# Loading and turning z earlier, and a regrouped start, in a gated attention kernel with a maxout layer

## The chip, the cores and the metric

The kernel runs on one core of a Trainium2 chip. The metric is the device time of one execution in microseconds, and lower is better. Five engines work beside each other: PE (TensorE, matrix products into PSUM), DVE (VectorE), ACT (ScalarE), POOL (GpSimd) and SP (SyncE). Here POOL and SP mostly issue transfers, each from a queue of its own that is served in order.

## The reference, cut to what matters

There are B = 8 sequences of S = 3072 rows. z has 64 columns, u and v have 256, and w1 and w2 are 256 x 1024.

```
scores = z @ z.T / S                     # one 3072 x 3072 matrix for each sequence
attn   = maximum(scores, 0) ** 2
x      = u * (attn @ v)
out    = maximum(x @ w1, x @ w2) @ w_out
```

scores is symmetric, so a block below the diagonal is a turned block from above it.

## The kernel before

**Tiles.** S is cut into 24 blocks of 128 rows, and four blocks make a chunk of 512 queries. One `Step` (b, s) does chunk s of sequence b, six for each sequence and 48 in all. A step adds up 24 blocks k of attn @ v into two PSUM tiles `xacc` (256 rows of D, 512 queries). Its result times u (`epilogue`, L299) is `xT`, which goes through the maxout layer (`d_ps`, `g_sb`, `o_ps`, `o_sb`) three steps later (LAG = 3), so that TensorE always has products at hand.

**Scores.** `scores_pair` (from L220 on) makes the scores of two blocks k0, k0 + 1 for the 512 queries of a step, from `zT`, the turned z: two products, run beside each other on the two halves of the rows. ACT takes the maximum with zero (`r_sb`, L233; DVE at L231 for two pairs of the head), DVE squares it (`a_sb`, L236). If the block lies above the diagonal, SP issues a DMA transpose of it (`aT`), which a later step of the same sequence uses; in the first sequence steps 0 to 3 compute each other's blocks directly instead (`direct`). From step 4 on the four diagonal blocks are made by `scores_diag`: only the upper half is computed and three small DMA transposes fill the rest (`aD`). `s_ps`, `d_ps`, `o_ps` and the transposes `tpz` of the start share three PSUM buffers (`mm_psum`).

**z.** For each sequence z is loaded by POOL (`load_z`, cast to bf16) and turned by two DMA transposes on SP (`make_zT`). The first sequence's z alone is turned by TensorE (`zT_pe`, L149), and its result is copied by DVE or ACT (L150).

**The planner.** `work` lists TensorE's products in order, with planned times from their lengths. Scores have no planned length: they are put in between as windows of up to three pairs (`scores_window`). Each window is placed, from the last to the first, at the last place that suits the due times of its tiles: the planned time of the first use less LAT_OWN, LAT_TURNED or LAT_DIAG (L536), or 2592 ns in the first steps. The three windows of the very start are written out by hand (`ahead`, `squared`, `third`), with products of zeros (`idle`) between them. `transfers` holds loads and transposes with planned times. A load is put behind a small copy on POOL (`gate`, L98) that waits for the newest square or other fresh result, so that it is not issued too early. A transpose is only queued on SP.

**Start.** Nine blocks of z (ZF) come through SP in fp32 and are cast by DVE and ACT, the other 15 come through POOL, then v in six groups of four blocks and u.

Of the kernel before, what the change touches and what calls it, by code (L numbers as in the profile page):

```python
# [11 lines left out]
def kernel(  # L12
# [19 lines left out]
    nc = tc.nc  # L32
    fp32 = mybir.dt.float32
    bf16 = mybir.dt.bfloat16
# [4 lines left out]
    dqk = z.shape[-1]  # L39
    Dff = moe_w1.shape[-1]  # L40

    P = 128
    H = P // 2
    NSB = S // P
    G = 4
    WIN = 3
    GW = G * P
# [10 lines left out]
    consts = ctx.enter_context(tc.tile_pool(name="consts", bufs=1))  # L58
    zepool = ctx.enter_context(tc.tile_pool(name="zepool", bufs=1))
# [11 lines left out]
    mm_psum = ctx.enter_context(tc.tile_pool(name="mm_psum", bufs=3, space=bass.MemoryType.PSUM))  # L71
    acc_psum = ctx.enter_context(tc.tile_pool(name="acc_psum", bufs=1, space=bass.MemoryType.PSUM))

    pin = tc.keep_in_program_order

    def matmul(*args, **kw):
        return pin(nc.tensor.matmul(*args, **kw))  # L77
# [13 lines left out]
    def sp_dma(**kw):  # L91
        pin(nc.sync.dma_start(**kw))
# [7 lines left out]
    def load(**kw):  # L100
        pin(nc.gpsimd.dma_start(**kw))  # L101
# [19 lines left out]
    def load_v(b, v_sb, t0, n):  # L121
        load(
            out=v_sb[:, ds(t0, n), :],
            in_=v[b].rearrange("(p t) d -> p t d", p=P)[:, ds(t0, n), :],
        )

    def load_u(b, c):
        u_sb = ulpool.tile([P, G, D], bf16, name="u_sb")
        load(
            out=u_sb,  # L130
            in_=u[b].rearrange("(p t) d -> p t d", p=P)[:, ds(c * G, G), :],
        )
        return u_sb
# [10 lines left out]
    def zT_pe(zT, z_sb, s0, n, tpz=None):  # L144
        flat = z_sb.rearrange("p t d -> p (t d)")
        if tpz is None:
            tpz = mm_psum.tile([P, 8, P], bf16, name="tpz", tag="mm")
        for j in range(n):
            pin(nc.tensor.transpose(tpz[:, j, :], flat[:, ds((s0 + j) * dqk, P)], ident))  # L149
        return lambda copy: pin(copy(zT[:, ds(s0, n), :], tpz[:, :n, :]))  # L150
# [68 lines left out]
    def scores_pair(b, s, k0):  # L219
        q = seqs[b]  # L220
        s_ps = mm_psum.tile([P, 2, GW], fp32, name="s_ps", tag="mm")
        for j in range(2):
            score(q, s_ps[:, j, :], j, k0 + j, s, 0, G)
        yield
        a_sb = apool.tile([P, 2, GW], bf16, name="a_sb")
        r_sb = apool.tile([P, 2, GW], bf16, name="r_sb", bufs=3)

        head = b == 0 and s == 0 and k0 < 12
        keep = pin if head else lambda ins: None
        if head and k0 in (2, 10):  # L230
            keep(nc.vector.tensor_single_scalar(out=r_sb, in_=s_ps, scalar=0.0, op=ALU.max))  # L231
        else:
            keep(nc.scalar.activation(r_sb, s_ps, AF.Relu))  # L233
        if head:
            yield
        keep(nc.vector.tensor_mul(a_sb, r_sb, r_sb))  # L236
        gj = k0 // G
        if gj > s and not direct(b, s, gj):
            if (s, gj) not in q.T:
                q.T[s, gj] = tpool.tile([P, G, G, P], bf16, name="aT")  # L240
            turn(
                q.T[s, gj][:, ds(k0 - G * gj, 2), :, :].rearrange("p k q x -> p (k q) x"),
                a_sb.rearrange("p j q -> p (j q)"),
            )
        yield a_sb
# [149 lines left out]


    q = seqs[0]
    ZF = 9
    blank = consts.tile([P, GW], bf16)
    pin(nc.vector.memset(blank, 0.0))  # L400
    zf = opool.tile([P, G, D], fp32, name="o_sb").rearrange("p t (n d) -> p (t n) d", d=dqk)
    z_in = z[0].rearrange("(p t) d -> p t d", p=P)
    sp_dma(out=zf[:, :ZF, :], in_=z_in[:, :ZF, :])
    ident = consts.tile([P, P], bf16)
    make_identity(nc, ident)
    z_sb_0 = zepool.tile([P, NSB + 2, dqk], bf16, name="z_sb")
    pin(nc.gpsimd.memset(z_sb_0[:, 0:1, :], 0.0))
    pin(nc.gpsimd.memset(z_sb_0[:, NSB + 1 : NSB + 2, :], 0.0))
    load(out=z_sb_0[:, 1 + ZF : 1 + NSB, :], in_=z_in[:, ZF:, :])
    pin(nc.vector.tensor_copy(z_sb_0[:, 1:6, :], zf[:, :5, :]))  # L410
    pin(nc.scalar.copy(z_sb_0[:, 6 : 1 + ZF, :], zf[:, 5:ZF, :]))
    q.v = new_v()
    for t0 in range(0, NSB, G):
        load_v(0, q.v, t0, G)
    q.u_sb[0] = load_u(0, 0)
    q.zT = zpool.tile([P, NSB + 1, P], bf16, name="zT")


# [111 lines left out]
    steps = [Step(b, s) for b in range(B) for s in range(NG)]  # L530
# [2 lines left out]


    work = []
    LAT_OWN, LAT_TURNED, LAT_DIAG = 3500, 9000, 12000  # L536

    def put(ns, shares, fn, reads=()):
        work.append((ns, shares, fn, reads))
# [9 lines left out]
    def put_block(st, k):  # L549
        row = NG * st.b + st.s  # L550
        if k // G in st.early:
            reads = [((NG * st.b + k // G, k0), LAT_TURNED) for k0 in (G * st.s, G * st.s + 2)]
            put(216, False, lambda: st.add_early(k), reads)
        elif k // G == st.s and st.diag:
            put(216, False, lambda: st.add_diag(k % G), [((row, None), LAT_DIAG)])
        else:
            put(216, False, lambda: st.add_own(k), [((row, k - k % 2), LAT_OWN)])

# [127 lines left out]
    while True:  # L686
# [4 lines left out]
            break  # L691
        windows.insert(0, [tiles.pop()])
        places.insert(0, i)
    firsts = [tiles[i : i + 2] for i in range(0, 6, 2)]
    firsts += [tiles[i : i + WIN] for i in range(6, len(tiles), WIN)]
    for rows in reversed(firsts):
        places.insert(0, lay(rows, GAP_FIRST))
    windows = firsts + windows
# [34 lines left out]
    for n, st in enumerate(steps):  # L733
        b, s = st.b, st.s
        if n + 1 < len(steps):
            nx = steps[n + 1]
            plan_load(b, s, 5 if st.halves else 2, lambda nx=nx: fetch_u(nx.b, nx.s))
        plan(b, s, 1, False, lambda b=b, s=s: turn_u(b, s))
        if s == 0 and b + 1 < B:
            c = b + 1  # L740
            if b == 0:
                z_at, zT_at = (3, 5), (4, 4)
                v_at = [(4, 8), (4, 14), (5, 1), (5, 6), (5, 11), (5, 15)]
            else:
                z_at, zT_at = (0, 7), (3, 3)
                v_at = [(s, 14) for s in range(NG)]
            plan_load(b, *z_at, lambda c=c: fetch_z(c))
            plan(b, *zT_at, False, lambda c=c: turn_z(c))
            for i, at in enumerate(v_at):
                plan_load(b, *at, lambda c=c, i=i: fetch_v(c, i))  # L750
# [7 lines left out]
    def scores_window(w):  # L758
        gens = []
        for n, k0 in windows[w]:  # L760
            st = steps[n]
            make = scores_diag(st.b, st.s) if k0 is None else scores_pair(st.b, st.s, k0)
            gens.append((st, k0, make))
        for st, k0, gen in gens:
            next(gen)
        for st, k0, gen in gens:
            st.scored[k0] = a = next(gen)
            fresh[0] = a[:, 0, 0:1] if k0 is not None else a[:, 0, 0, 0:1]
# [3 lines left out]

    def idle(n):
        for _ in range(n):
            matmul(steps[0].xacc[0], blank[:, :P], blank, start=True, stop=True)


    laid = {i: [w for w in ws if w > 2] for i, ws in laid.items()}
    idle(6)
    parts = [zT_pe(q.zT, z_sb_0, 0, 5), zT_pe(q.zT, z_sb_0, 5, ZF - 5)]  # L780
    for part, copy in zip(parts, (nc.vector.tensor_copy, nc.scalar.copy)):
        part(copy)
    idle(4)
    heads = {k0: scores_pair(0, 0, k0) for w in range(3) for _, k0 in windows[w]}

    def ahead(*k0s):
        for k0 in k0s:
            next(heads[k0])

    def squared(*k0s):  # L790
        for k0 in k0s:
            steps[0].scored[k0] = a = next(heads[k0])
            fresh[0] = a[:, 0, 0:1]

    ahead(0, 2)
    ahead(0, 2)
    tpz = mm_psum.tile([P, 2, 8, P], bf16, name="tpz", tag="mm")
    parts = [zT_pe(q.zT, z_sb_0, ZF + 8 * i, 8, tpz[:, i]) for i in range(2)]
    squared(0)
    for part, copy in zip(parts, (nc.scalar.copy, nc.vector.tensor_copy)):  # L800
        part(copy)
    ahead(4)
    idle(1)
    ahead(6)
    idle(2)
    ahead(4, 6)
    squared(2, 4)

    def third():
        ahead(8, 10)  # L810
        ahead(8, 10)
        squared(6, 8, 10)

    laid.setdefault(spots[0] + 2, []).insert(0, -1)
    for i, (_, _, fn, _) in enumerate(work):
        for w in laid.get(i, []):
            scores_window(w) if w >= 0 else third()
        while transfers and transfers[0][0] <= begins[i]:
            _, _, is_load, begin_transfer = transfers.pop(0)
            if is_load:  # L820
                gate(fresh[0])
            begin_transfer()
        fn()
# [30 lines left out]
```

## Time and profile before

| | us |
|---|---|
| median of 3 runs | 977.18 (976.05 to 978.23) |
| profiled execution | 974.66 |
| its span in the trace | 972.9 |
| PE busy in the span | 956.9 |
| ACT busy | 485.9 |
| DVE busy | 391.5 |

PE is busy for 98% of the span. The rest of the profile is read stretch by stretch: a wait of PE is named with what ended it last, and times are microseconds from the start of the span. The granted clock of the profiled run is 0.996 as a mean.

### The profile page before, as it was taken

To read this page: it belongs to the slowest core of one execution; us is meant where nothing else is said; L and a number is where in the kernel's file an instruction comes from. 1 tells how busy PE (TensorE), PEld (TensorE's weight loads), DVE (VectorE), ACT (ScalarE), POOL (GpSimd) and SP (SyncE) were. 2 spreads that over 40 slices of the span, in tenths; PEclk is the share of its full clock that TensorE was granted. 3 is DMA by queue.
4 is the path that set the end of the run, shared out by engine and by line. 5 is a ranking of instruction groups with operands and counts; after the bars stand their busy time and mean duration, and the time that the engine had idled before them with its cause. 6 is when DMAs were issued, how large, how long until landed. Compare 5 with 4: busy or idle time off the path is not lost.

```text
span 972.9 us, 24379 instructions
## 1 busy us (share of the span) xinstructions
PE 956.9 (98%) x10446; PEld 590.5 (61%) x10446; DVE 391.5 (40%) x648; ACT 485.9 (50%) x533; POOL 78.9 (8%) x228
## 2 busy tenths in 40 slices
PE   8996999999999999999999999999999999999998
PEld 3353655676667666666666666666666666666666
DVE  5662344334532454325433344333444333442211
ACT  6863445445553555445554454544555545554323
POOL 2110110000000001000010001000000000000000
PEclk9998999999999999999999999999999999999999
DMA  8997999989999899997998989978899889875411
GB/s 138 152 155 141 161 157 185 156 134 174 111 178 172 129 196 131 158 184 132 168 168 141 170 147 147 194 132 153 144 155 190 152 138 168 153 139 112 102 42 66
DMA packets 378557, 144.07 MB, mean 148 GB/s; under 512 B 356945, under 2 KB 358609, under 8 KB 378449
## 3 DMA queue, kind: packets, MB, share of 16 engines
q1 hardware_dynamic: 361888, 112.78, 66.0%
q0 software_dynamic: 16560, 29.74, 23.3%
q8 instruction: 81, 1.33, 0.6%
q14 instruction: 28, 0.22, 0.1%
HBM read 59.77 MB, written 25.17 MB: 87 GB/s over the span
## 4 chain that ended last, share of the span: by engine, by line
PE 96%; DMA 2%; DVE 1%; ACT 1%; issue 0%; SPq 0%; POOL 0%; DVEq 0%; POOLq 0%
PE xacc L77 51%; PE o_ps L77 22%; PE d_ps L77 16%; PE s_ps L77 7%; DMA v_sb<-in_v_dram 1%; DMA zT<-z_sb 1%; ACT r_sb L233 0%; DMA o_sb<-in_z_dram 0%; DVE g_sb L513 0%; PE tpz L149 0%; DVE a_sb L236 0%; PE w2o_ps L77 0%; DVE r_sb L231 0%; ACT r_sb L261 0%; ACT zT L150 0%
## 5 line engine op out<-in xcount | busy, mean ns | idle before, releaser
L77 PEld LDWEIGHTS <-v_sb 64*128 64x128 bf16 (+1 forms) x4416 | 255.5, 94 | 232.9 <-issue 8.3
L233 ACT ACTIVATE r_sb<-s_ps 128x1024 bf16<-128x1024 f32 x258 | 260.7, 1024 | 161.9 <-PE s_ps L77 159.1
L236 DVE TENSOR_TENSOR a_sb<-r_sb 128x1024 bf16<-128x1024 bf16 x260 | 179.4, 691 | 398.2 <-ACT r_sb L233 395.1
L77 PE MATMUL xacc<-a_sb,v_sb 64*128 64x512 bf16 (+1 forms) x1888 | 254.0, 377 | 1.2 <-DMA v_sb<-in_v_dram 1.0
L77 PE MATMUL xacc<-aT,v_sb 64*128 64x512 bf16 x1824 | 228.8, 376 | 0.0
L77 PE MATMUL o_ps<-w_out_sb,g_sb 64*128 64x256 bf16 (+1 forms) x3008 | 202.0, 269 | 0.4 <-ACT g_sb L513 0.2
L77 PE MATMUL d_ps<-xT,w_sb 64*128 64x512 bf16 (+1 forms) x1520 | 191.1, 376 | 0.2 <-ACT g_sb L513 0.2
L513 ACT ACTIVATE g_sb<-d_ps 128x1024 bf16<-128x1024 f32 x127 | 124.8, 1021 | 107.9 <-PE d_ps L77 105.2
L77 PEld LDWEIGHTS <-g_sb 64*128 64x128 bf16 (+1 forms) x3008 | 166.6, 94 | 11.8 <-issue 1.0
L77 PEld LDWEIGHTS <-w_sb 64*128 64x128 bf16 (+1 forms) x1520 | 85.5, 94 | 77.9 <-issue 1.3
L527 ACT COPY o_sb<-o_ps 128x512 f32<-128x512 f32 x92 | 53.8, 585 | 150.8 <-PE o_ps L77 150.8
L77 PE MATMUL s_ps<-zT 64*128 64x512 bf16 (+3 forms) x696 | 117.5, 357 | 9.1 <-DMA zT<-z_sb 7.9
L77 PE MATMUL xacc<-aD,v_sb 64*128 64x512 bf16 x704 | 92.2, 378 | 0.0
L513 DVE TENSOR_SCALAR g_sb<-d_ps 128x1024 bf16<-128x1024 f32 x61 | 74.7, 1225 | 39.9 <-PE d_ps L77 31.2
L77 PE MATMUL o_ps<-W2o_sb,xT 64*128 64x256 bf16 (+1 forms) x752 | 76.0, 269 | 0.0
L263 DVE TENSOR_SCALAR r_sb<-s_ps 128x384 bf16<-128x384 f32 x44 | 24.5, 558 | 112.3 <-PE s_ps L77 112.3
L77 PEld LDWEIGHTS <-zT 64*128 64x128 bf16 x696 | 37.3, 94 | 50.3 <-issue 9.3
L299 DVE SCALAR_TENSOR_TENSOR xT<-xacc,uT 128x512 bf16<-128x512 f32 x96 | 61.9, 683 | 14.5 <-PE xacc L77 14.5
L261 ACT ACTIVATE r_sb<-s_ps 128x896 bf16<-128x896 f32 x44 | 40.3, 917 | 49.8 <-PE s_ps L77 49.1
L98 POOL COPY gate_sb<-a_sb 128x1 bf16<-128x1 bf16 x75 | 14.4, 192 | 582.5 <-DVE a_sb L236 404.4
L77 PEld LDWEIGHTS <-xT 64*128 64x128 bf16 (+1 forms) x752 | 42.2, 94 | 0.4
L101 POOL DMA_DIRECT2D u_sb<-in_u_dram x48 | 25.5, 531 | 18.3 <-issue 17.6
(40 smaller groups left out, 127.8 us busy)
## 6 DMA issues: line engine op xcount, KB each, us to landing
out_dram<-o_sb SPq DMA_DIRECT2D x47, 512.0 KB, 3.4
v_sb<-in_v_dram POOLq DMA_DIRECT2D x48, 256.0 KB, 5.4
u_sb<-in_u_dram POOLq DMA_DIRECT2D x48, 256.0 KB, 5.2
aT<-a_sb SPq DMA_TRANSPOSE x228, 4.9
z_sb<-in_z_dram POOLq DMA_DIRECT2D x7, 384.0 KB, 8.8
aD<-aD SPq DMA_TRANSPOSE x132, 3.7
w_sb<-in_moe_w_dram POOLq DMA_DIRECT2D x2, 512.0 KB, 7.7
uT<-u_sb SPq DMA_TRANSPOSE x48, 3.8
```

Source lines behind the costliest of these rows:

```text
L77: return pin(nc.tensor.matmul(*args, **kw))
L98: pin(nc.gpsimd.tensor_copy(gate_sb, tile_ap))
L101: pin(nc.gpsimd.dma_start(**kw))
L233: keep(nc.scalar.activation(r_sb, s_ps, AF.Relu))
L236: keep(nc.vector.tensor_mul(a_sb, r_sb, r_sb))
L261: nc.scalar.activation(r_sb, s_ps[:, 0:7, :], AF.Relu)
L263: nc.vector.tensor_single_scalar(out=r2_sb, in_=s2_ps[:, 2:5, :], scalar=0.0, op=ALU.max)
L299: nc.vector.scalar_tensor_tensor(out=xT[:, dc, :].rearrange("p (t q) -> p t q", q=P), in0=xacc[dc].rearrange("p (t q) -> p t q", q=P), sca ...
L513: nc.any.tensor_single_scalar(out=g_sb, in_=d_ps, scalar=0.0, op=ALU.max)
L527: nc.any.tensor_copy(o_sb[:, ds(t, 2), :], o_ps[:, :, :D])
```

## The change

The sequence's z and the diagonal:

- the load of the second sequence's z is planned for 6 us into step (0, 2) instead of 5 us into (0, 3), and its two transposes for 8 us into step (0, 3) instead of 4 us into (0, 4);
- the diagonal groups of the first sequence are due 9500 instead of 12000 ns before their use.

The start:

- five blocks of z come through SP, eight through POOL in front of all v, and the last eleven behind the first group of v; u and the last two groups of v change places;
- TensorE turns z in three parts of 5, 8 and 12 blocks, copied by DVE, ACT and DVE;
- the zero products are half as wide (256 columns), 18 instead of 13 of them;
- the first windows hold 2, 1 and 3 pairs instead of 2, 2 and 2, and the relu of pair 10 goes from DVE to ACT.

With it the planner's places become (planned us of `work`):

| | before | after |
|---|---|---|
| window of (0, 1), pairs 0 to 4 | 5.2 | 7.8 |
| window of (0, 2), pairs 18 to 22 | 23.3 | 25.9 |
| window of (0, 3), pairs 12 to 16 | 31.1 | 33.7 |
| window of (0, 3), pairs 18 to 22 | 33.7 | 40.6 |
| diagonal of (0, 4), with pair 20 | 40.6 | 49.4 |
| diagonal of (0, 5) | 56.3 | 56.3 |
| diagonal of (1, 0) | 58.0 | 58.0 |
| load of z for sequence 1 | 36.1 | 26.7 |
| its transposes | 55.1 | 39.1 |

Step (0, 4) begins at 51.1. Every window between the first rows is one place later, and from the diagonal of (0, 5) on nothing moves.

```diff
--- before.py
+++ after.py
@@ -144,7 +144,7 @@
     def zT_pe(zT, z_sb, s0, n, tpz=None):
         flat = z_sb.rearrange("p t d -> p (t d)")
         if tpz is None:
-            tpz = mm_psum.tile([P, 8, P], bf16, name="tpz", tag="mm")
+            tpz = mm_psum.tile([P, n, P], bf16, name="tpz", tag="mm")
         for j in range(n):
             pin(nc.tensor.transpose(tpz[:, j, :], flat[:, ds((s0 + j) * dqk, P)], ident))
         return lambda copy: pin(copy(zT[:, ds(s0, n), :], tpz[:, :n, :]))
@@ -227,7 +227,7 @@
 
         head = b == 0 and s == 0 and k0 < 12
         keep = pin if head else lambda ins: None
-        if head and k0 in (2, 10):
+        if head and k0 == 2:
             keep(nc.vector.tensor_single_scalar(out=r_sb, in_=s_ps, scalar=0.0, op=ALU.max))
         else:
             keep(nc.scalar.activation(r_sb, s_ps, AF.Relu))
@@ -395,24 +395,32 @@
 
 
     q = seqs[0]
-    ZF = 9
-    blank = consts.tile([P, GW], bf16)
-    pin(nc.vector.memset(blank, 0.0))
+    ZF, ZP = 5, 13
+    blank = consts.tile([P, 2 * P], bf16)
     zf = opool.tile([P, G, D], fp32, name="o_sb").rearrange("p t (n d) -> p (t n) d", d=dqk)
+    z_sb_0 = zepool.tile([P, NSB + 2, dqk], bf16, name="z_sb")
     z_in = z[0].rearrange("(p t) d -> p t d", p=P)
+
+    def load_z_0(t0, n):
+        load(out=z_sb_0[:, ds(1 + t0, n), :], in_=z_in[:, ds(t0, n), :])
+
     sp_dma(out=zf[:, :ZF, :], in_=z_in[:, :ZF, :])
+    load_z_0(ZF, ZP - ZF)
     ident = consts.tile([P, P], bf16)
     make_identity(nc, ident)
-    z_sb_0 = zepool.tile([P, NSB + 2, dqk], bf16, name="z_sb")
-    pin(nc.gpsimd.memset(z_sb_0[:, 0:1, :], 0.0))
-    pin(nc.gpsimd.memset(z_sb_0[:, NSB + 1 : NSB + 2, :], 0.0))
-    load(out=z_sb_0[:, 1 + ZF : 1 + NSB, :], in_=z_in[:, ZF:, :])
-    pin(nc.vector.tensor_copy(z_sb_0[:, 1:6, :], zf[:, :5, :]))
-    pin(nc.scalar.copy(z_sb_0[:, 6 : 1 + ZF, :], zf[:, 5:ZF, :]))
+    pin(nc.vector.memset(blank, 0.0))
+    pin(nc.vector.memset(z_sb_0[:, 0:1, :], 0.0))
+    pin(nc.vector.memset(z_sb_0[:, NSB + 1 : NSB + 2, :], 0.0))
+    pin(nc.vector.tensor_copy(z_sb_0[:, 1:4, :], zf[:, :3, :]))
+    pin(nc.scalar.copy(z_sb_0[:, 4 : 1 + ZF, :], zf[:, 3:ZF, :]))
     q.v = new_v()
-    for t0 in range(0, NSB, G):
+    load_v(0, q.v, 0, G)
+    load_z_0(ZP, NSB - ZP)
+    for t0 in range(G, 4 * G, G):
         load_v(0, q.v, t0, G)
     q.u_sb[0] = load_u(0, 0)
+    for t0 in range(4 * G, NSB, G):
+        load_v(0, q.v, t0, G)
     q.zT = zpool.tile([P, NSB + 1, P], bf16, name="zT")
 
 
@@ -533,7 +541,7 @@
 
 
     work = []
-    LAT_OWN, LAT_TURNED, LAT_DIAG = 3500, 9000, 12000
+    LAT_OWN, LAT_TURNED, LAT_DIAG_0, LAT_DIAG = 3500, 9000, 9500, 12000
 
     def put(ns, shares, fn, reads=()):
         work.append((ns, shares, fn, reads))
@@ -552,7 +560,7 @@
             reads = [((NG * st.b + k // G, k0), LAT_TURNED) for k0 in (G * st.s, G * st.s + 2)]
             put(216, False, lambda: st.add_early(k), reads)
         elif k // G == st.s and st.diag:
-            put(216, False, lambda: st.add_diag(k % G), [((row, None), LAT_DIAG)])
+            put(216, False, lambda: st.add_diag(k % G), [((row, None), LAT_DIAG if st.b else LAT_DIAG_0)])
         else:
             put(216, False, lambda: st.add_own(k), [((row, k - k % 2), LAT_OWN)])
 
@@ -691,8 +699,8 @@
             break
         windows.insert(0, [tiles.pop()])
         places.insert(0, i)
-    firsts = [tiles[i : i + 2] for i in range(0, 6, 2)]
-    firsts += [tiles[i : i + WIN] for i in range(6, len(tiles), WIN)]
+    firsts = [tiles[:2], tiles[2:3]]
+    firsts += [tiles[i : i + WIN] for i in range(3, len(tiles), WIN)]
     for rows in reversed(firsts):
         places.insert(0, lay(rows, GAP_FIRST))
     windows = firsts + windows
@@ -739,7 +747,7 @@
         if s == 0 and b + 1 < B:
             c = b + 1
             if b == 0:
-                z_at, zT_at = (3, 5), (4, 4)
+                z_at, zT_at = (2, 6), (3, 8)
                 v_at = [(4, 8), (4, 14), (5, 1), (5, 6), (5, 11), (5, 15)]
             else:
                 z_at, zT_at = (0, 7), (3, 3)
@@ -772,15 +780,13 @@
 
     def idle(n):
         for _ in range(n):
-            matmul(steps[0].xacc[0], blank[:, :P], blank, start=True, stop=True)
-
-
-    laid = {i: [w for w in ws if w > 2] for i, ws in laid.items()}
-    idle(6)
-    parts = [zT_pe(q.zT, z_sb_0, 0, 5), zT_pe(q.zT, z_sb_0, 5, ZF - 5)]
-    for part, copy in zip(parts, (nc.vector.tensor_copy, nc.scalar.copy)):
-        part(copy)
-    idle(4)
+            matmul(steps[0].xacc[0][:, : 2 * P], blank[:, :P], blank, start=True, stop=True)
+
+
+
+    laid = {i: [w for w in ws if w > 4] for i, ws in laid.items()}
+    for k, w in ((2, -2), (4, -1), (8, 3), (14, 4)):
+        laid.setdefault(spots[0] + k, []).insert(0, w)
     heads = {k0: scores_pair(0, 0, k0) for w in range(3) for _, k0 in windows[w]}
 
     def ahead(*k0s):
@@ -792,29 +798,31 @@
             steps[0].scored[k0] = a = next(heads[k0])
             fresh[0] = a[:, 0, 0:1]
 
+    idle(10)
+    zT_pe(q.zT, z_sb_0, 0, ZF)(nc.vector.tensor_copy)
+    idle(3)
     ahead(0, 2)
     ahead(0, 2)
-    tpz = mm_psum.tile([P, 2, 8, P], bf16, name="tpz", tag="mm")
-    parts = [zT_pe(q.zT, z_sb_0, ZF + 8 * i, 8, tpz[:, i]) for i in range(2)]
+    part = zT_pe(q.zT, z_sb_0, ZF, ZP - ZF)
+    idle(5)
     squared(0)
-    for part, copy in zip(parts, (nc.scalar.copy, nc.vector.tensor_copy)):
-        part(copy)
+    part(nc.scalar.copy)
     ahead(4)
-    idle(1)
-    ahead(6)
-    idle(2)
-    ahead(4, 6)
-    squared(2, 4)
+    ahead(4)
+    squared(2)
 
     def third():
-        ahead(8, 10)
-        ahead(8, 10)
-        squared(6, 8, 10)
-
-    laid.setdefault(spots[0] + 2, []).insert(0, -1)
+        ahead(6, 8, 10)
+        ahead(6, 8, 10)
+        squared(4, 6)
+
+    def fourth():
+        zT_pe(q.zT, z_sb_0, ZP, NSB + 1 - ZP)(nc.vector.tensor_copy)
+        squared(8, 10)
+
     for i, (_, _, fn, _) in enumerate(work):
         for w in laid.get(i, []):
-            scores_window(w) if w >= 0 else third()
+            scores_window(w) if w >= 0 else fourth() if w + 1 == 0 else third()
         while transfers and transfers[0][0] <= begins[i]:
             _, _, is_load, begin_transfer = transfers.pop(0)
             if is_load:
```

## Prediction

> **What bounds the kernel now.** I read the page's summary first, then TensorE's waits, then the timeline around the longest of them.
>
> ```profile
> span 972.9 us, 24379 instructions
> PE 956.9 (98%) x10446; PEld 590.5 (61%) x10446; DVE 391.5 (40%) x648; ACT 485.9 (50%) x533; POOL 78.9 (8%) x228
> PE s_ps L77 <- DMA zT<-z_sb: 7.9, 1, 7.9
> PE xacc L77 <- DMA v_sb<-in_v_dram: 1.0, 1, 1.0
> ```
>
> TensorE is busy for 98% of the span, so only what empties or slows TensorE can move the time. Half of its 16 us of idle time is one wait: the scores of the second sequence wait 7.9 us for the turned z. No other wait in that list is above about 1 us, and most lie in the first 17 us. The timeline of that wait, and the granted clock (the number before the last two) in stretches around it:
>
> ```profile
> 62.61 0.53 POOL L101 DMA_DIRECT2D z_sb<-in_z_dram  x1 [0.26 <-issue]
> 62.13 10.82 SPq L92 DMA_TRANSPOSE aT<-a_sb  x3
> 73.04 3.77 SPq L92 DMA_TRANSPOSE aD<-aD  x3
> 81.76 0.43 PE L77 MATMUL s_ps<-zT 64*128 64x512 bf16 x4
> 82.03 0.60 PE L77 MATMUL d_ps<-xT,w_sb 64*128 64x512 bf16 x4
> 83.35 3.96 SPq L92 DMA_TRANSPOSE zT<-z_sb  x2
> 91.80 0.71 PE L77 MATMUL s_ps<-zT 64*128 64x512 bf16 x4 [7.88 <-DMA zT<-z_sb]
> 92.31 1.91 PE L77 MATMUL xacc<-a_sb,v_sb 64*128 64x512 bf16 x8
> 94.02 1.54 PE L77 MATMUL xacc<-aD,v_sb 64*128 64x512 bf16 x8
> 95.40 0.38 PE L77 MATMUL s_ps<-zT 64*128 64x512 bf16 x2
> 60.00:65.00 5.00, 5.00 (x25) 2.20 (x23) 3.69 (x4) 2.79 (x3) 0.96 (x4) 1.00 1.45 129
> 92.00:96.00 4.00, 4.00 (x30) 1.78 (x28) 1.64 (x5) 1.09 (x2) 0.71 (x2) 0.62 0.32 40
> ```
>
> The z load starts at 62.61, but its two transposes stand in SP's queue behind ten other entries (the three aT and three aD above among them) and are issued only at 83.35, while TensorE wants the result at 91.80 - 7.88 = 83.92. They land some 8 us later. The stall then costs a second time: the granted clock in the 4 us after it is 0.62.
>
> **The change: z sooner (L742).** Price of the stall: 7.88 us of waiting, and the slow clock behind it. From 91.80 to 95.40 TensorE does a group of four diagonal scores and sixteen products. At full clock the four scores take 82.03 - 81.76 = 0.27, and sixteen products 2 x 0.87, by this pair of groups of eight:
>
> ```profile
> 103.00 1.02 PE L77 MATMUL xacc<-aT,v_sb 64*128 64x512 bf16 x8
> 103.87 1.02 PE L77 MATMUL xacc<-a_sb,v_sb 64*128 64x512 bf16 x8
> ```
>
> That is 2.0 of the 3.6 us, so 1.6 us were lost to the clock (4 x (1 - 0.62) = 1.5 says the same). The stall is worth 7.9 + 1.6 = 9.5 us, and both go together, since nothing else idles TensorE so long.
>
> Does it go? The load is planned at 26.7 instead of 36.1 (planned us, without the scores) and is gated by the last square of the window at 25.9. The rows for it:
>
> ```profile
> z_sb<-in_z_dram POOLq DMA_DIRECT2D x7, 384.0 KB, 8.8
> aD<-aD SPq DMA_TRANSPOSE x132, 3.7
> 47.03 0.76 PE s_ps L77 x6
> 53.86 0.82 PE L77 MATMUL s_ps<-zT 64*128 64x512 bf16 x6
> 57.18 0.69 DVE L236 TENSOR_TENSOR a_sb<-r_sb 128x1024 bf16<-128x1024 bf16 x1 [0.22 <-ACT r_sb L233]
> 76.35 2.76 PE L77 MATMUL d_ps<-xT,w_sb 64*128 64x512 bf16 x24
> ```
>
> That window starts at 47.03 in the trace (third row, from the chain), and a window's last square ends some 4.0 us after its start (53.86 to 57.18 + 0.69). Less one window put off (0.76) and the head's gain (near 2, below), that is 48.3, so POOL issues near 49. At the median of 8.8 us to landing z is there at 58. The last entry in front of the transposes is now one aT. Its window follows the one at 53.86 after 0.76 + 2.69 (head, below), at 57.3, less the same 2.8: 54.5, and squared by 58.5. SP then issues zT from about 60 to 64, and with the 8 us of before it has landed by 72. TensorE wants it at 83.92 - 2 = 82. With 10 us to spare nothing remains of the wait.
>
> What is late next? **The diagonal of step 4 (LAT_DIAG_0).** Its window moves from planned 40.6 to 49.4, the last place before step 4. Before, its transposes were issued at 73.04 and used at 94.02, a margin the stall gave. Now its scores stand before the last eight products (1.7) ahead of the row of 76.35: 76.35 - 1.7 - 0.5 for themselves - 2 for the head is 72. ACT and DVE need 2 us, SP issues the three transposes from 74 to 77.8 behind the output of step 0, and they land 3.7 later, 78 to 81.5. TensorE wants the first at 83.92 + 0.27 + 0.87 + 0.22 = 85.3, less some 2 for the head: 83.3, and the last 0.4 later. Two us to spare: cost nothing, but this is the thinnest cover. If SP is backed up it costs what it is late, us for us. The other items in front of it on SP are the two zT (3.96 to issue) and three aT, which took 10.82 in the crowded stretch at 62 (DMA share 1.45); z's own load has left that stretch. The v wait of 1.0 us at step 6 is gated by products a fixed distance ahead, so it stays, give or take 1.
>
> **The head.** TensorE's start before (two rows of the chain and two of the list of transfers at the end):
>
> ```profile
> 0.74 0.39 SPq L92 DMA_DIRECT2D o_sb<-in_z_dram  x1
> 1.20 2.74 PE L77 MATMUL xacc<-blank 128*128 128x512 bf16 x6 [1.20 <-DVE blank L400]
> 3.80 0.33 DVE L410 CAST z_sb<-o_sb 128x320 bf16<-128x320 f32 x1 [2.67 <-DMA o_sb<-in_z_dram]
> 4.28 1.12 PE L149 MATMUL tpz<-ident,z_sb 128*128 128x128 bf16 x9 [0.34 <-DVE z_sb L410]
> 5.00 0.49 DVE L150 COPY zT<-tpz 128x640 bf16<-128x640 bf16 x1 [0.88 <-PE tpz L149]
> 5.19 1.59 PE L77 MATMUL xacc<-blank 128*128 128x512 bf16 x4
> 6.71 0.61 PE L77 MATMUL s_ps<-zT 64*128 64x512 bf16 x4
> 7.14 1.02 ACT L233 ACTIVATE r_sb<-s_ps 128x1024 bf16<-128x1024 f32 x1 [1.12 <-PE s_ps L77]
> 7.25 1.07 PE L149 MATMUL tpz<-ident,z_sb 128*128 128x128 bf16 x16
> 7.36 1.23 DVE L231 TENSOR_SCALAR r_sb<-s_ps 128x1024 bf16<-128x1024 f32 x1 [1.86 <-PE s_ps L77]
> 8.50 0.68 DVE L236 TENSOR_TENSOR a_sb<-r_sb 128x1024 bf16<-128x1024 bf16 x1
> 11.58 1.04 PE L77 MATMUL xacc<-a_sb,v_sb 128*128 128x512 bf16 x4
> 20.18 2.69 PE xacc L77 x12
> 26.33 0.76 PE s_ps L77 x6
> o_sb<-in_z_dram SPq DMA_DIRECT2D x1, 288.0 KB, 3.0
> out_dram<-o_sb SPq DMA_DIRECT2D x4, 128.0 KB, 1.7
> ```
>
> First load: 160 KB instead of 288. It lies between the 1.7 us of a 128 KB transfer and the 3.06 measured here (0.74 to 3.80); I take 2.5, nearer the row of the same load, so z lands at 3.3. Cast to transposes was 0.48; the cast shrinks by two fifths, so 0.4. Five transposes to the end of their copy: 5.00 + 0.49 - 4.28 = 1.21, the same 640 columns. Three half-wide zero products (1.59 / 4 / 2 = 0.2 each) end before that. First scores at about 4.95, not 6.71, where four wide zero products still held them. At the slow clock of the zero products a pair takes some 0.5, so ACT starts at 5.6, DVE's r for pair 2 runs 6.1 to 7.35 and the first square is ready at 8.05. TensorE meanwhile does eight transposes, five zero products (1.0) and pair 4, whose zT waits for ACT's copy (near 7.9): first product at 8.25, not 11.58.
>
> It owes more then. Per pair of scores the chain gives 0.76 / 3 = 0.25 us, per twelve products 2.69, per transpose 1.07 / 16 = 0.067. Up to the end of step 0 it does 48 products (10.76), twelve pairs (3.04, the first window of step 1 among them) and twelve transposes (0.80): 14.6. One window (0.76) is put off, since L694 now cuts the first windows 2, 1, 3. Without waits the same point comes at 8.25 + 14.6 + 0.76 = 23.6, against 26.33. Before, 14.75 us held 48 products and eleven pairs, 13.5, so 1.2 us were waits for squares and buffers. After, I see two: the third transposes want a PSUM buffer that ACT still reads, and so does the third pair of the step 1 window. I take 1.0. **Head: 2.7 - 1.0 = 1.7 us sooner**, from 0 to 2.6.
>
> Edits that cost nothing: L227 moves one r from DVE (1.23) to ACT (1.02), in a stretch where squares wait for ACT; it is inside the 1.0. POOL's 256 KB of v now stand between two z loads; the third part of z is wanted only near 11, covered by the products of k = 0 to 3. Steps 1 to 3 have one window of lead less: a pair is squared 2.3 to 4.0 us after its window starts and is wanted 3.45 (0.76 + 2.69) or more after it. The pair wanted first is the one ready first, so no wait; without that cover a step's first pair is late by at most the one r in front of it, 1.0.
>
> **Sum:** 9.5 + 1.7 = 11.2 us. The profiled execution took 974.66 (972.9 span, 1.8 around it) and comes to 963.5. It lies 2.5 below the median of the runs, 977.18, and the prediction is for such a median: 966.0. What a measurement of this kernel can tell from no change is 0.2%, 2 us.
>
> **Rivals.** *The clock comes late.* The work at 6.71 ran fast because TensorE had been nearly full since 1.20. Now ten half-wide products end near 3.3 and a gap of about 0.4 and five transposes follow. If full speed comes some 3.4 us later, near 10 (after the stall it took from 91.80 to about 95), then eight transposes (0.54), five zero products (0.54), a pair (0.25) and some four products (0.87) take twice their time, 2.2 us more, of which 0.7 falls into waits that are there anyway: the head gains 0.2 and the time is 967.5. For it: less work in that stretch; against it: before, a gap of 0.34 did no harm. 0.2. The Trainium skill ("TensorE: Matmul & The Clock Gate", Part 1) speaks for this rival: full clock comes only after a whole busy window of about 3.4 us, which runs free of the kernel's start, so a thinner start can miss one; the 0.62 after the stall agrees with that. Its Part 4 adds that transposes do not count as activity. No run here shows that yet, and by it the start, with only 2.2 us of zero products before the gap, would more often miss: 967.5 instead of 966.0.
>
> *The diagonal of step 4 lands late*, as priced above, by about 3 us: 969.0. For it: SP took 10.82 us for three aT once; against it: z's load no longer shares that stretch. 0.14.
>
> *The stall stays*, because zT is issued no sooner than SP's earlier entries allow: then only the head counts, 975.5. Against it: between z's load and its transposes SP now has one uT and one aT, not ten entries. 0.03.
>
> *Slower: SP's head is blocked.* The zT pair now stands before three aT, an output and the step 4 diagonal. If z lands late, all of them wait, TensorE with them, and the clock falls. It needs the diagonal past 83.3 + 9.6 = 93 (9.6 + 1.6 is the whole gain). With z landing near 72 and aT and zT at 3.6 us each, 18 for the five, it lands at 90 + 0.5 + 3.8 + 3.7 = 98, a wait of 14.7: 966.0 + 14.7 + 1.6 = 982. For it: SP is first in, first out, and DMA is full there; against it: z would have to take 22 us. 0.06.
>
> **Numbers.** The forecast has 0.57. Its own range is 963.5 to 968 (a head of 0 is 967.7). The range reaches up through the late clock and the late diagonal, with its price uncertain by 1.5, to 970.5; down, to a head at its best (0.9 more) and no v wait (1.0), 964.1, less 0.6 for the spread of the runs. Faster: 0.57 + 0.2 + 0.14 = 0.91; same 0.03; slower 0.06.
>
> **What would show it.** The wait for zT gone from TensorE's waits and the clock at 1.00 from 80 on; zT issued near 60 and landed before 72; first scores near 5.0 and first products near 8.3; step 0's epilogue some 2.5 us sooner and the window after it caught up by step 4. It is wrong if xacc waits for aD near 83, if SP shows zT after 75, or if the scores at 5 are still at half speed at 10.

## The result, and the profile after

The changed kernel takes 961.12 us (median of 4 runs, 961.01 to 961.23), against 977.5 for four runs of before: a ratio of 0.9834, 95% interval 0.9817 to 0.9851. The prediction said 966.0, 963.5 to 970.5. The direction held, and so did the mechanism of the largest term, the stall; the gain is larger than the range allows. With the experiments below came 57 more runs of before. All 61 lie between 972.81 and 980.53 with a median of 975.75, so the four were high, and the gain is nearer 14.6 us than 16.4. The profiled executions differ by 13.4 us: 974.66 before, 961.23 after.

The page's head and TensorE's waits after, each with total us, count and longest:

```profile
span 959.5 us, 24383 instructions
PE 952.9 (99%) x10444; PEld 586.4 (61%) x10451; DVE 390.7 (41%) x649; ACT 486.3 (51%) x533; POOL 79.7 (8%) x227
PE xacc L77 <- DVE blank L411: 1.1, 1, 1.1
PE s_ps L77 <- ACT zT L150: 0.6, 1, 0.6
PE xacc L77 <- DVE a_sb L236: 0.3, 1, 0.3
PE d_ps L77 <- ACT g_sb L521: 0.2, 1, 0.2
PE o_ps L77 <- ACT g_sb L521: 0.2, 1, 0.2
```

The wait for zT is gone, and with it the wait for v, which the prediction had left in place. TensorE idles 6.6 us (959.5 - 952.9), not 16. The timeline after shows why:

```profile
48.93 0.53 POOL L101 DMA_DIRECT2D z_sb<-in_z_dram  x1
58.20 5.49 SPq L92 DMA_TRANSPOSE aT<-a_sb  x1
63.80 4.83 SPq L92 DMA_TRANSPOSE zT<-z_sb  x2
68.73 4.05 SPq L92 DMA_TRANSPOSE aT<-a_sb  x3
72.87 0.53 SPq L92 DMA_DIRECT2D out_dram<-o_sb  x1
73.49 3.91 SPq L92 DMA_TRANSPOSE aD<-aD  x3
```

z is loaded at 48.93 (forecast 49). zT is issued at 63.80, 20 us sooner than before; forecast was 60, but one aT in front took 5.49 us to issue. The step 4 diagonal goes out from 73.49 to 77.4 (forecast 74 to 77.8), and nothing waits for it.

Three places of the chain, first before, then after, show where the time came from: step 4's first d_ps group, the o_ps group behind the stall, and the o_ps group behind the v wait.

```profile
76.42 2.70 PE d_ps L77 x24
95.78 4.37 PE o_ps L77 x74
136.46 4.37 PE o_ps L77 x80
```

```profile
23.11 0.76 PE s_ps L77 x6
73.92 2.70 PE d_ps L77 x24
83.63 4.37 PE o_ps L77 x80
123.07 4.37 PE o_ps L77 x80
```

The lead is 2.50 us at step 4, 12.15 behind the stall and 13.39 behind the v wait; the remaining 836 us add nothing. So the start gave 2.5, the stall 9.65, and the v wait and some slightly slow products round it 1.24. At the start the window at 23.11 is the one put off; with its 0.76 the point that before reached at 26.33 comes at 23.87, 2.46 sooner.

### The profile page after: what moved, and what is told of

It reads as the page before. It is cut to its first block, busy times and chain, and to the rows that moved or that the text cites. A ratio compares the mean times of both kernels' runs of the same rounds, so it can differ in the third digit from the quotient of the medians.

```text
span 959.5 us, 24383 instructions
## 1 busy us (share of the span) xinstructions
PE 952.9 (99%) x10444; PEld 586.4 (61%) x10451; DVE 390.7 (41%) x649; ACT 486.3 (51%) x533; POOL 79.7 (8%) x227
## 4 chain that ended last, share of the span: by engine, by line
PE 98%; DVE 1%; issue 0%; ACT 0%; DVEq 0%; ACTq 0%
PE xacc L77 52%; PE o_ps L77 22%; PE d_ps L77 17%; PE s_ps L77 7%; DVE g_sb L521 0%; ACT r_sb L233 0%; PE w2o_ps L77 0%; PE tpz L149 0%; DVE r_sb L231 0%; DVE a_sb L236 0%; ACT o_sb L535 0%; DVE o_sb L348 0%; DVE blank L411 0%; DVEq L521 0%; ACTq L233 0%
## 5 line engine op out<-in xcount | busy, mean ns | idle before, releaser
L77 PEld LDWEIGHTS <-v_sb 64*128 64x128 bf16 (+1 forms) x4416 | 252.4, 94 | 233.2 <-issue 6.4
```

## The experiments

The medians, in us. "z" is the sooner z (L742), "diagonal" the later due time, "start" everything else. Each kernel ran beside before on the same chip, and the ratios below are to those runs. The new start without the later due time was not run.

| kernel | z | diagonal | start | median | runs |
|---|---|---|---|---|---|
| before | | | | 975.75 | 61, 972.81 to 980.53 |
| diagonal alone | | x | | 973.22 | 12, 971.36 to 977.30 |
| diagonal and start | | x | x | 972.78 | 12, 970.98 to 975.17 |
| z alone | x | | | 963.95 | 5, 963.64 to 965.79 |
| z and diagonal | x | x | | 961.88 | 5, 961.16 to 964.63 |
| after | x | x | x | 961.1 | 8, 960.55 to 961.23 |

**z and the diagonal in the old start.**

```diff
-                z_at, zT_at = (3, 5), (4, 4)
+                z_at, zT_at = (2, 6), (3, 8)
-            put(216, False, lambda: st.add_diag(k % G), [((row, None), LAT_DIAG)])
+            put(216, False, lambda: st.add_diag(k % G), [((row, None), LAT_DIAG if st.b else 9500)])
```

> The kernel before with the sooner z and the later diagonal alone, the start as it was. The profiled executions differ by 13.4 us, the medians by 16.4; 3 us lie between the profile of before and its own runs, and after has no such gap. Theory A (the gap belongs to the stall: how long the clock stays slow behind it differs from run to run, and the profiled run was a short one): the whole stall goes, 9.7 us in the profile, the 1 us wait for v with it, and the gap too: near 964, all runs within 0.3 of each other. Theory B (the gap belongs to the start, where the clock comes at another time in each run): 977.5 - 10.7 = 967, and the runs still spread over some 2 us.

Measured: 961.88, ratio 0.9853 (0.9828 to 0.9879). That is not within 0.3 from run to run, but four of five runs lie within 1 us, and the time is far below the 967 of theory B. It is also 2 us below the 964 of theory A, which gave nothing to the diagonal. The surprise is how little the whole new start still has to give: 0.8 us. Its chain:

```profile
23.32 0.75 PE s_ps L77 x6
74.13 2.70 PE d_ps L77 x24
```

With the old start the window at step 1 begins at 23.32, against 23.11 with the new one, and 22.67 in a second profile of the new one.

**z alone.** The first of the two edits above, without the second.

> The kernel before with the sooner z alone; the diagonal keeps its due time of 12000, so its window stays at planned 40.6. My theory: the later diagonal gains nothing by itself, since TensorE has slack for it in both places: the same time as with both, within 0.3. Rival: with both, SP's queue is eased by taking the three aD behind three aT; without that zT and aD come together and TensorE waits for one of them, 1 to 4 us slower than with both.

Measured: 963.95, ratio 0.9874 (0.985 to 0.9898), 2.1 us slower than with both. My theory falls, but so does the rival: in its profile TensorE waits neither for zT nor for aD. The 2 us are lost in the first 17 us of the chain, which is that of before:

```profile
14.75 1.23 DVE r_sb L231
16.63 2.75 PE xacc L77 x12
76.36 2.70 PE d_ps L77 x24
```

So the later due time acts on the start. The planner lays windows backward from the last: with the diagonal allowed later, every window before it moves one place later, and pairs 12 to 16 of step 0 no longer stand in front of the first products. It does so in the old start as in the new one: with the old due time it puts the first window of (0, 1) at planned 5.2 in both, with the later one at 7.8 in both.

**The diagonal alone, and the start with the old z.** The first is before with the second edit of the first experiment and nothing else. The second is this:

```diff
 after, for the start with the old z:
-                z_at, zT_at = (2, 6), (3, 8)
+                z_at, zT_at = (3, 5), (4, 4)
```

> The kernel before with the later due time of the diagonal groups alone; z is loaded and turned as before. If this edit gains only by the order of windows at the start, the 2.1 us that it gave beside the sooner z come here too: 973.5, with the stall and its spread unchanged. If it gained by SP's order around the sooner transposes, nothing comes without them: 975.6.

> The changed kernel with the times of z and its transposes as before: the new start and the later diagonal alone. In the profile the window at step 1 comes 2.5 us sooner than before and the wait for zT of some 8 us is back. Theory A: 977.5 - 2.5 = 975, and the runs spread over some 2 us as before's do. Theory B: 972 to 973, with runs close together.

Measured: 973.22 (ratio 0.9975, 0.9958 to 0.9992) and 972.78 (0.9963, 0.9947 to 0.9978). The later diagonal gives 2.5 us where z stays late, 2.1 where it does not, so it needs no sooner zT. The new start adds 0.4 to it, less than the runs of either spread. In both the wait for zT is back, 7.3 us in each profile, and so is the spread of the runs, 6 and 4 us: theory A in this point, since the start is the new one in the second kernel. The time of the second is not A's 975 but what theory B had, 972 to 973; A's figure started from 977.5, and from the median of all runs of before it would be about 973.

**The windows moved by hand.** Before, with the sooner z; the diagonal of step 4 stays at planned 40.6.

```diff
+    places[3:17] = places[4:17] + [spots[[begins[i] for i in spots].index(39744)]]
     laid = {}
```

> The kernel before with the sooner z, the diagonal's due time as it was, and by hand the order of windows that the later diagonal brings: windows 12 to 16 of step 0 and the thirteen behind it each one place later, the window of (0, 3), pairs 18 to 22 at planned 39.7; the diagonal of step 4 stays at 40.6. The theory now: the later diagonal gains through the start alone, because three pairs no longer stand in front of TensorE's first products: 961.9, as with the later due time. Rival: it gains by SP's order around the diagonal: 964, as without.

Measured: 963.29 in six runs, ratio 0.9883 (0.9858 to 0.9908); four at 962.51 to 963.41 and two at 967. The median alone decides nothing. The profile does:

```profile
4.30 0.66 PE tpz L149 x9
22.45 0.75 PE s_ps L77 x6
61.69 0.88 ACT r_sb L233
63.67 0.39 PE s_ps L77 x2
74.60 2.70 PE d_ps L77 x24
```

The window at step 1 begins at 22.45 without any change of the due time, so the order of windows makes the gain. It is not all of the 3.9 us against before's 26.33: in this execution the nine transposes of the start take 0.66 us, and 1.12 in before (4.28 in the prediction's rows), and the first scores come at 5.82 instead of 6.78. About 1 us is thus work that ran faster there, not the order, and 22.45 with that added is close to the 23.32 of the later due time. About 1.3 us of the gain are given back near 61, where the two windows that I set side by side wait for ACT: from the window at step 1 to step 4's first d_ps group it is 52.15 us here and 50.81 with the later due time. Without those the four runs stand near 961.8. The two longer runs, one of them the profiled one, have a wait of their own, shown further below.

**Zero products in the stall.** Before, with 30 zero products while TensorE waits for zT.

```diff
     def scores_window(w):
         gens = []
+        if [r for r in windows[w]] == [(NG, None)]:
+            warm = mm_psum.tile([P, 2, GW], fp32, name="warm", tag="mm")
+            for _ in range(30):
+                matmul(warm[:, 0, :], blank[:, :P], blank, start=True, stop=True)
```

> The kernel before with 30 products of zeros (6.5 us at full clock) into a score buffer that nobody reads, put into the stall before the diagonal scores of the second sequence. The wait for zT stays; only the idle time of TensorE goes. If the 1.6 us behind the stall is the clock's, the profile is 1.6 shorter: 973. Theory A: the runs lose the gap as well, near 973 with a spread under 0.5. Theory B: runs near 976, spread as before. Rival to both: the slow products after the stall are slow for another reason (operands, contention), and nothing changes: 977.5.

Measured: 972.51 in 12 runs, ratio 0.9964 (0.9947 to 0.9981): 3 us faster, with a mean granted clock of 0.998 to 1.0 in every run, where the runs of before beside it have 0.993 to 0.996. The wait for zT is still there: the zero products fill 6.65 us of it, and 1.13 remain. Theory A is right on the clock and wrong on the spread, which stays at 6 us: so the clock is not what makes the runs of before differ most. The profiled run of this kernel, at 975.44, lies 3 us above its median and holds the longest v wait of all, 2.9 us, so that wait may be a part of it. The zero products, and the granted clock (the number before the last two) in the same four microseconds here and in the start with the old z:

```profile
82.91 6.65 PE L77 MATMUL warm<-blank 128*128 128x512 bf16 x29
88.00:92.00 4.00, 2.87 (x22) 1.20 (x21) 0.79 (x2) 0.89 (x1) 0.00 (x0) 1.00 0.85 180
88.00:92.00 4.00, 3.80 (x20) 1.57 (x22) 1.63 (x5) 0.92 (x1) 0.71 (x2) 0.50 0.24 49
```

Five profiles of the same stretch, from the end of the stall to the first o_ps group on W2o, the product of w2 and w_out (this kernel; before; the start with the old z; the late transposes of the next part; the diagonal alone):

```profile
90.68 0.45 PE L77 MATMUL s_ps<-zT 64*128 64x512 bf16 x4 [1.13 <-DMA zT<-z_sb]
93.78 0.38 PE L77 MATMUL o_ps<-W2o_sb,xT 64*128 64x256 bf16 x4
```

```profile
96.49 0.38 PE L77 MATMUL o_ps<-W2o_sb,xT 64*128 64x256 bf16 x4
```

```profile
88.20 0.72 PE L77 MATMUL s_ps<-zT 64*128 64x512 bf16 x4 [7.28 <-DMA zT<-z_sb]
94.25 0.38 PE L77 MATMUL o_ps<-W2o_sb,xT 64*128 64x256 bf16 x4
```

```profile
88.17 0.71 PE L77 MATMUL s_ps<-zT 64*128 64x512 bf16 x4 [7.31 <-DMA zT<-z_sb]
93.72 0.38 PE L77 MATMUL o_ps<-W2o_sb,xT 64*128 64x256 bf16 x4
```

```profile
89.24 0.71 PE L77 MATMUL s_ps<-zT 64*128 64x512 bf16 x4 [7.32 <-DMA zT<-z_sb]
94.35 0.38 PE L77 MATMUL o_ps<-W2o_sb,xT 64*128 64x256 bf16 x4
```

The stretch takes 3.10 us with a full clock, and 4.69 (96.49 less the 91.80 of the prediction), 6.05, 5.55 and 5.11 behind a stall. A stall of 7.3 to 7.9 us costs 1.6, 2.95, 2.45 or 2.0 us of clock, and the profile that the prediction read was the cheapest of the four. The Trainium skill ("TensorE: Matmul & The Clock Gate", Part 1) has the clock return at the end of a free-running window of some 3.4 us, so that the price hangs on where the stall ends in it. These rows agree: at a granted clock of 0.50 a price of 1.6 to 2.95 us is 3.2 to 5.9 us of slow work, about one to two such windows.

**Load or transposes.** After, with one of the two times put back at a time.

```diff
 late transposes:
-                z_at, zT_at = (2, 6), (3, 8)
+                z_at, zT_at = (2, 6), (4, 4)
 late load:
-                z_at, zT_at = (2, 6), (3, 8)
+                z_at, zT_at = (3, 5), (3, 8)
```

> The changed kernel with the two transposes of z back at 4 us into step (0, 4), the load left early. My theory: the stall of before was made by the place of the transposes in SP's queue, not by the load: SP reaches them only after the squares of step 4, near 81, so TensorE waits some 7 us again and the time is that of the new start with the old z, 972 to 973. Rival: the load was the cause (its 8.8 us ran into the crowded stretch near 62): with the load early the transposes land in 4 us, the wait is 3 us or less and the clock does not fall, 965.

> The changed kernel with the load of z back at 5 us into step (0, 3), the transposes left early: they now stand in SP's queue before z has come, and block it. By the prediction's rival (SP's head is blocked) z lands near 69, so zT is issued from 69 to 74 and lands near 80, just in time for TensorE at 81.4; the three aT, the output and the step 4 diagonal come 6 us later, the diagonal near 84 to 86, where TensorE wants it at 83.1 to 83.5: a wait of 1 to 3 us, 962 to 964. If SP catches up as it did in the changed kernel (three aT in 4.05 us), there is no wait: 961.2.

Measured: 972.85 with late transposes (12 runs, ratio 0.9971, 0.9954 to 0.9988), all of the stall; 961.28 with the late load (6 runs, 0.9875, 0.9841 to 0.9909), none of it. SP's queue, first with the late transposes, then with the late load:

```profile
79.28 1.29 SPq L92 DMA_TRANSPOSE aT<-a_sb  x1
80.68 3.92 SPq L92 DMA_TRANSPOSE zT<-z_sb  x2
```

```profile
64.49 3.42 SPq L92 DMA_TRANSPOSE zT<-z_sb  x2
68.00 4.40 SPq L92 DMA_TRANSPOSE aT<-a_sb  x3
73.22 3.83 SPq L92 DMA_TRANSPOSE aD<-aD  x3
```

The place of the transposes in SP's queue was the cause, and the load sooner was not needed for the median. With the late load SP stands idle until z has landed, but POOL issues it at 59.27, SP goes on at 64.49, and three aT then take 4.40: SP catches up. In this profile, and by their times in three more of the six runs, a blocked SP does no harm. The other two took 966.86 and 970.46; they have no trace, and whether the blocked SP is the reason stays open.

**No zero products.** After, with `idle` doing nothing.

```diff
-        for _ in range(n):
+        for _ in range(0):
```

> The changed kernel without its 18 products of zeros, which change no result. If they keep the clock up, as the rival on a late clock has it, TensorE starts its transposes at 3.3 with nothing before them, the full clock comes some 2 to 3.4 us later, near 8 to 9, the products from 8 on run slowly for a while, and the window at step 1 comes 1 to 2 us later: 962 to 963. If they are idle work that nothing depends on, 961.1.

Measured: 963.36, ratio 0.9872 (0.9848 to 0.9897), 2.3 us slower than after. From its timeline:

```profile
3.37 0.71 PE L149 MATMUL tpz<-ident,z_sb 128*128 128x128 bf16 x5 [3.37 <-DVE z_sb L414]
8.31 1.89 PE L77 MATMUL xacc<-a_sb,v_sb 128*128 128x512 bf16 x4
10.13 1.24 PE L77 MATMUL s_ps<-zT 64*128 64x512 bf16 x6
```

Four products take 1.82 us (8.31 to 10.13); the four at 8.14 in the changed kernel take 0.97, to 9.11. The granted clock reads 1.00 in both, so at the start a slow clock is read from these lengths alone. So the zero products earn their place: the rival of the late clock is a real mechanism with a price of about 2, but in the changed kernel the products at 8.14 were already fast.

**After once more, and two tries to beat it.**

```diff
 relu of pair 20 on DVE:
-        if head and k0 == 2:
+        if b == 0 and s == 0 and k0 in (2, 20):
 first v before the identity:
     load_z_0(ZF, ZP - ZF)
+    q.v = new_v()
+    load_v(0, q.v, 0, G)
     ident = consts.tile([P, P], bf16)
     ...
-    q.v = new_v()
-    load_v(0, q.v, 0, G)
     load_z_0(ZP, NSB - ZP)
```

> The changed kernel unaltered, beside the three below and more runs of before on the same chip. The median of before was 977.5 in four runs and 975.5 to 975.8 in two sets of 23 and 17. If the part of the gain above the profiles' 13.4 us came from those four runs, the changed kernel stays at 961.1 and the gain is 14.5. If it differs from chip to chip, both move.

> The changed kernel with the relu of pair 20 of the first step on DVE instead of ACT. In the changed kernel's profile the third pair of the window at 19.3 waits some 0.4 us for ACT to free its score buffer. If ACT is what holds the start there, this gains 0.3 to 0.4: 960.8. If DVE's slower 1.23 us only takes ACT's place, 961.1 to 961.5.

> The changed kernel with the first group of v issued before POOL builds the identity, 0.5 us sooner. In the changed kernel's profile the first products at 8.14 wait for that group last, their squares are there at 7.5. If so they start near 7.7 and the whole start comes 0.4 sooner: 960.7. If ACT's chain of relus holds the start anyway, 961.1.

Measured on one chip, beside before at 975.64: after 961.08 (ratio 0.9844, 0.9823 to 0.9865), pair 20 on DVE 960.71 (0.9847, 0.9826 to 0.9867), v sooner 960.96 (0.9846, 0.9825 to 0.9867). After repeats, so the extra gain of the first measurement came from the four runs of before. With pair 20 on DVE the split of the window at the start closes (the second profile of after, whose first products come at 7.70, then this kernel, with 7.68):

```profile
16.31 0.34 PE s_ps L77 x2
19.58 0.39 PE s_ps L77 x2
```

```profile
16.29 0.75 PE s_ps L77 x6
18.87 0.76 PE s_ps L77 x6
```

Four of its five runs are at 960.33 to 961.20, the fifth at 963.44; the 0.4 us is as forecast but hardly beyond the spread of the runs. The next window begins at 22.32 instead of 22.67. With v sooner the first products come at 7.85, between the 8.14 and 7.70 of the two profiles of after, and the third pair still waits for ACT until 19.73 (20.02 and 19.58): nothing gained, ACT holds the start.

## Why the prediction was wrong in size

**The stall (9.5): right.** 9.65 in the profiles. The place of the transposes in SP's queue, not the load's, did it.

**The v wait ("stays, give or take 1"): wrong.** The wait for this load is in the profiles with late transposes (before 1.0, diagonal alone 0.2, diagonal and start 1.6, late transposes 0.8, zero products in the stall 2.9 us) and in none with early ones. The prediction held the load to be a fixed distance ahead, and its issue is: some 10 us ahead of the place of its use before and after (123.35 to 133.34, and 111.15 to 120.97). What changed is how long it takes to land (last column, before and after):

```profile
v_sb<-in_v_dram POOLq DMA_DIRECT2D x1, 256.0 KB, 11.0
```

```profile
v_sb<-in_v_dram POOLq DMA_DIRECT2D x1, 256.0 KB, 4.6
```

The five profiles with late transposes have 10.2 to 12.8 there, and their waits are what goes beyond those 10; those with early ones have 4.5 to 5.8, and 8.8 in the long run of the windows moved by hand. That the late zT pair, and what it pushes back on SP, slow that load is suggested by this; it was not tried by itself. The wait and the slightly slow products round it are 1.2 us of the error.

**The head (1.7): too small by 0.8, and mostly for the wrong edit.** It is 2.5 in the profile above, and 2.9 in the second one of after, where step 4's first d_ps group begins at 73.48. First scores at 4.61 (forecast 4.95) and first products at 8.14 (8.25) came as worked out, but I put 1.0 for later waits, where the profile leaves about 0.4. More important, I took the window put off for a work of L694 and the gain for that of the new loads. The sum fits the changed kernel, since it counts the windows in their new order; which edit made that order was wrong. The diagonal's due time puts the windows off, and alone in the old start gives 2.1 to 2.5; the new start gives 0.4 to 0.8 on top of it, and by itself was not tried. The sum has the clue: before, three pairs stood in front of the first products and waited for ACT.

**The base (977.18 - 974.66 = 2.5, carried over): wrong, half the error.** The profile after comes to 961.23, where the steps said 963.5; the other 2.6 us are this term. I treated the gap between profile and median as belonging to any kernel. In the changed kernel the median lies 0.1 below its profiled execution. In before, 1.4 of the 2.5 is the choice of three runs from a kernel whose runs differ by 8 us; the changed kernel's eight differ by 0.7. The other 1.1 is the median of 61 runs above the profile. The 0.4 to 1.4 us of clock that the profile of before saved against the three others behind a stall are of that size; that they are the reason is not shown, since the runs spread about as far without the slow clock.

**The rivals.** The diagonal did not come late, the stall did not stay, and SP caught up. The late clock came in a small part: four scores at 4.61 still took 1.04 us, 0.60 in the second profile, and the first products came at 8.14 and 7.70. That is 0.4 us, not the rival's 2.2.

## What to carry to other kernels

The stall of the matrix engine here was paid twice, in waiting and in slow clock behind it, and the second part differed from profile to profile: price such a stall from several profiles. The spread of the runs shrank from 8 us to 0.7 when the stall went, though not when the slow clock alone was taken away, and a median of few runs of a kernel with such a spread is a poor base. For a transfer that comes late, look at its place in its queue before its load. Where a planner lays work out backward, one due time moves everything before it: read the new order from end to end before giving a gain to an edit.

## What the runs showed that I had not expected

Among the kernels with early transposes single runs are 2 to 9 us longer than the rest of their kernel. The one that a profile caught (windows moved by hand) waits for the uT of a step, its turned u:

```profile
PE xacc L77 <- DVE xT L299: 3.9, 1, 3.9
111.91 8.17 SPq L92 DMA_TRANSPOSE aT<-a_sb  x2
124.03 15.02 DMA uT<-u_sb
```

Two aT took 8.17 us to issue, against 4.60 for the same pair in the changed kernel, and the uT behind them 15.0 to land. SP's queue near the end of the first sequence is thus the next place to look; why its transposes slow down in some runs is open.
